# Interleaving the two output tiles of attention-times-V, and moving four x transposes to other buffers and places

## The chip, the cores and the metric

The kernel runs on one core of one Trainium2 chip. The metric is device microseconds of one execution. The profile's span is about 1.7 us shorter than the time of the same execution (339.8 us against 341.54), so spans are compared with spans and times with times. In the profile lines PE is TensorE (matmuls), PEld its weight loads, DVE VectorE, ACT ScalarE, POOL GpSimd and SP the engine that issues DMAs; L354 is line 354 of the kernel. The "granted clock" is the share of full speed that TensorE was allowed, 1 being all of it.

## The reference

Sliding-window attention (window 32, 8 batches, 8 heads, 576 positions, head size 64) gives x; a gated FFN follows.

```python
def _attn_ref(q, k, v):                      # each [8, 8, 576, 64], float32
    scores = np.matmul(q, k.transpose(0, 1, 3, 2)) / np.sqrt(64)
    mask = np.abs(pos[:, None] - pos[None, :]) <= 32
    scores = np.where(mask, scores, -1e9)
    attn = softmax(scores)                   # cut: max, exp, sum
    return np.matmul(attn, v)

def _moe_ref(x, w_gate, w_val, w_out):       # x [4608, 512], d_ff 1536
    g = x @ w_gate
    silu = g * (1.0 / (1.0 + np.exp(-g)))
    return (silu * (x @ w_val)) @ w_out
```

## The kernel before

The tokens are cut into 9 chunks of 512. For each chunk j the kernel runs FFN1 (96 matmuls with a 128x512 output into `gv_ps`), then FFN2 (48 into `ob`, in eight half-steps of six), and slips the attention of the next tokens between the half-steps. Attention works on "pairs": two blocks of 64 queries. `pair_scores` computes scores and their exponential, VectorE multiplies by the mask, `pair_av` multiplies by V, VectorE normalises to x, and `pair_xt` turns x round for the next FFN1, by a DMA transpose or, at the start of the kernel, by TensorE.

```python
ps_a = ...  # 2 buffers of two PSUM banks: scores, gv_ps, the second AV of two ("score buffers")
ps_c = ...  # 1 buffer of two banks: AV
ps_o = ...  # 2 buffers of one bank: ob, and x transposes by TensorE ("output buffers")

def pair_av(m, pool=None):
    p = pts.pop(m)
    o = (pool or ps_c).tile([128, 2, 512], FP32, ...)
    for i in range(2):                       # i: which of the two query blocks
        b, t = divmod(2 * m + i, NT)
        for h in range(H):
            nc.tensor.matmul(
                out=o[64 * i:64 * i + 64, h // 4, 66 * (h % 4):66 * (h % 4) + 66],
                lhsT=p[:, place(b, h)[0], i, place(b, h)[1], :],
                rhs=v16[b % 2][:, t, h, :], start=True, stop=True)
    ...                                      # VectorE: reciprocal, multiply -> x16s[m]

def pair_xt(m, on_pe=False):
    ...
    if not on_pe:
        nc.sync.dma_start_transpose(out=dst, in_=x16)
        return
    tp = ps_o.tile([128, GS, 128], FP16, tag="o", name="xt_ps")
    for g in range(GS):
        nc.tensor.transpose(out=tp[:, g, :], in_=x16[:, 128 * g:128 * g + 128], identity=ident)
    cast_act(dst, tp)                        # ScalarE copy to SBUF

# end of FFN2 of chunk 0
ffn2_sub(0, 2, 0); pair_scores(8); ffn2_sub(0, 2, 1)
pair_av(6); pair_av(7, ps_a)
ffn2_sub(0, 3, 0)
pair_xt(4, True)
ffn2_sub(0, 3, 1)                            # the last half-step; then osb <- ob on ScalarE
pair_xt(5, True); pair_xt(6, True); pair_xt(7, True)
pair_av(8, ps_a)
pair_xt(8)
```

(`...` marks cuts.) A "bank" in this text is 128x512 float32 of PSUM as this program allocates it: half of a score buffer or of the AV buffer, or one output buffer. With i outside, all eight matmuls that write output partitions 0 to 63 come first in the program, then the eight that write 64 to 127. The first group is called tile A below, the second tile B. Each matmul of AV uses 128 rows and 64 columns of the array (`128*64` in the lines of the trace, where an FFN matmul has `128*128`).

## Time and profile before

| | before |
|---|---|
| time, median of three runs (lowest to highest) | 341.29 us (341.18 to 341.92) |
| span of the profiled execution | 339.8 us |
| TensorE busy | 96% of the span |
| TensorE in the chain that ended last | 94% |
| granted TensorE clock | 0.995 |

The page of the kernel before, the busy line of its part 1 and the chain of its part 4 (shares of the span by engine, then by engine, tile and line):

```profile
PE 327.0 (96%) x2592; PEld 159.8 (47%) x2592; DVE 157.9 (46%) x288; ACT 155.9 (46%) x223; POOL 106.6 (31%) x139
...
PE 94%; DVE 1%; ACT 1%; DMA 1%; issue 1%; POOL 0%; POOLq 0%
PE gv_ps L391 55%; PE ob L405 27%; PE o_ps L354 4%; PE s_ps L306 3%; PE warm L437 2%; PE qk_ps L281 1%; ACT xT L262 1%; DMA xT<-x_1758 1%; PE ob L424 1%; DVE p_t L344 1%; DVE v_103 L265 0%; PE xt_ps L378 0%; DVE mask L202 0%; ACT osb L413 0%; DVE osb_4022 L265 0%
```

TensorE binds nearly everywhere, so a microsecond of TensorE work is worth up to a microsecond. AV (`o_ps`) is 4% of the chain. But "busy" does not tell whether those matmuls overlap; the order of starts does.

The timeline of TensorE before, around the AV of pairs 4 and 5 (start in us, duration, engine, line, operation, output<-inputs, count; neighbours are merged). In pair 4 the two tiles read different V buffers, so they can be told apart: tile A reads `v_103`, tile B `v_104`:

```profile
50.84 0.34 PE L354 MATMUL o_ps<-v_103,p_t 128*64 128x66 f16 x5
51.00 0.22 PE L354 MATMUL o_ps<-v_104,p_t 128*64 128x66 f16 x1
51.02 0.20 PE L354 MATMUL o_ps<-v_103,p_t 128*64 128x66 f16 x1
51.05 0.20 PE L354 MATMUL o_ps<-v_104,p_t 128*64 128x66 f16 x1
51.06 0.19 PE L354 MATMUL o_ps<-v_103,p_t 128*64 128x66 f16 x1
51.09 0.19 PE L354 MATMUL o_ps<-v_104,p_t 128*64 128x66 f16 x1
51.09 0.19 PE L354 MATMUL o_ps<-v_103,p_t 128*64 128x66 f16 x1
51.12 0.64 PE L354 MATMUL o_ps<-v_104,p_t 128*64 128x66 f16 x21
51.69 1.47 PE L405 MATMUL ob<-wo_128,hT 128*128 128x512 f16 x6
```

Five matmuls of tile A start alone, then the last three of A and the first three of B start in alternation. So in this trace the two tiles already run at once in part, for three matmuls of eight. Tile B's first matmul (51.00 us) starts ahead of tile A's sixth, seventh and eighth (51.02, 51.06 and 51.09 us), which stand before it in the kernel's loops: across the two tiles the order of starts was not the program's here.

The timeline at the end of the first FFN2, before (only TensorE, ScalarE and VectorE lines are copied; the bracket is idle time and what ended it):

```profile
57.12 0.69 DVE L363 TENSOR_TENSOR x_910<-o_ps,rall 128x512 f16<-128x512 f32 x1
...
57.22 1.46 PE L405 MATMUL ob<-wo_128,hT 128*128 128x512 f16 x6
57.42 0.60 ACT L262 ACTIVATE xT<-xt_ps 128x512 f16<-128x512 f16 x1 [1.52 <-PE xt_ps L378]
...
58.51 0.39 PE L378 MATMUL xt_ps<-ident,x_834 128*128 128x128 f16 x4
...
59.07 0.60 ACT L413 ACTIVATE osb<-ob 128x512 f32<-128x512 f32 x1 [1.06 <-PE xt_ps L378]
59.56 1.66 ACT L262 ACTIVATE xT<-xt_ps 128x512 f16<-128x512 f16 x3
59.72 0.38 PE L378 MATMUL xt_ps<-ident,x_890 128*128 128x128 f16 x4 [0.82 <-ACT osb L413]
...
61.28 1.02 PE L391 MATMUL gv_ps<-xT,wg_126 128*128 128x512 f16 x4 [0.15 <-ACT xT L262]
```

`x_910` is the normalised x of pair 7 (ready at 57.12 + 0.69 = 57.81 us), `x_834` that of pair 5, `x_890` that of pair 6. After the last half-step ScalarE copies the output (`osb`), then three turned x tiles, while TensorE mostly waits; FFN1 of chunk 1 starts at 61.28 us.

### The profile page before, as it was taken

The page shows a single profiled execution, that of the slowest core. Times are in us where ns is not written, and L with a number is a line of the kernel's source. Part 1 is how long each engine was busy: PE and PEld are TensorE (multiplying, and loading weights), DVE is VectorE, ACT ScalarE, POOL GpSimd, SP SyncE. Part 2 cuts the span into 40 slices and gives each one's busy share as a digit, 9 for nine tenths or more (in the row PEclk, how much of TensorE's full clock was granted, in tenths as well). Part 3 has the DMA queues.
Part 4 walks back from the last instruction along what each step waited for, and adds up shares of the span by engine and source line. Part 5 has one row for each costly group of instructions (what it writes and reads, how often), then busy time and mean ns, then how long its engine had stood idle before and what let it go on. Part 6 is the DMA issues. An engine that isn't in the chain of part 4 may idle for free.

```text
span 339.8 us, 6448 instructions
## 1 busy us (share of the span) xinstructions
PE 327.0 (96%) x2592; PEld 159.8 (47%) x2592; DVE 157.9 (46%) x288; ACT 155.9 (46%) x223; POOL 106.6 (31%) x139
## 2 busy tenths in 40 slices
PE   6889999999999999999999999999999999999993
PEld 3444545444544454445444454455445544444442
DVE  3744365336624763466345644564446634403310
ACT  2964576535543464337333743373336443223321
POOL 8973875146204710463045503560000000000000
PEclk9999999999999999999999999999999999999997
DMA  7999999799969996999599949998530420020012
GB/s 274 169 212 301 212 158 200 126 131 111 147 148 149 99 136 138 131 129 129 151 125 127 130 122 130 152 108 150 111 62 33 106 65 1 33 93 0 2 63 70
DMA packets 152981, 41.92 MB, mean 123 GB/s; under 512 B 140528, under 2 KB 146416, under 8 KB 152944
## 3 DMA queue, kind: packets, MB, share of 16 engines
q0 software_dynamic: 100640, 16.52, 67.7%
q1 hardware_dynamic: 52304, 24.92, 31.4%
q8 instruction: 22, 0.36, 0.5%
q14 instruction: 15, 0.12, 0.1%
HBM read 37.75 MB, written 9.44 MB: 139 GB/s over the span
## 4 chain that ended last, share of the span: by engine, by line
PE 94%; DVE 1%; ACT 1%; DMA 1%; issue 1%; POOL 0%; POOLq 0%
PE gv_ps L391 55%; PE ob L405 27%; PE o_ps L354 4%; PE s_ps L306 3%; PE warm L437 2%; PE qk_ps L281 1%; ACT xT L262 1%; DMA xT<-x_1758 1%; PE ob L424 1%; DVE p_t L344 1%; DVE v_103 L265 0%; PE xt_ps L378 0%; DVE mask L202 0%; ACT osb L413 0%; DVE osb_4022 L265 0%
## 5 line engine op out<-in xcount | busy, mean ns | idle before, releaser
L398 DVE TENSOR_TENSOR hT<-ssb,gv_ps 128x512 f16<-128x512 f16 x108 | 74.3, 688 | 122.4 <-ACT ssb L397 122.1
L397 ACT ACTIVATE ssb<-gv_ps 128x512 f16<-128x512 f32 x108 | 64.5, 597 | 112.7 <-PE gv_ps L391 110.4
L391 PE MATMUL gv_ps<-xT,wg_126 128*128 128x512 f16 x432 | 110.8, 379 | 1.2 <-ACT xT L262 0.8
L391 PE MATMUL gv_ps<-xT,wv_127 128*128 128x512 f16 x432 | 110.9, 379 | 0.0
L405 PE MATMUL ob<-wo_128,hT 128*128 128x512 f16 x420 | 97.3, 380 | 0.0
L391 PEld LDWEIGHTS <-wv_127 128*128 128x128 f16 x432 | 42.3, 98 | 51.0
L391 PEld LDWEIGHTS <-wg_126 128*128 128x128 f16 x432 | 41.9, 98 | 51.6 <-issue 2.8
L405 PEld LDWEIGHTS <-hT 128*128 128x128 f16 x420 | 38.6, 98 | 43.6
L223 POOL DMA_DIRECT2D tok<-in_q_dram x30 | 25.4, 847 | 83.3 <-DMA qT_101<-tok 45.9
L312 ACT ACTIVATE p_t<-s_ps 128x1024 f16<-128x1024 f32 (+1 forms) x40 | 35.3, 937 | 12.3 <-PE s_ps L306 12.2
L413 ACT ACTIVATE osb<-ob 128x512 f32<-128x512 f32 x35 | 21.0, 600 | 41.7 <-PE ob L405 40.6
L223 POOL DMA_DIRECT2D tok<-in_k_dram x30 | 25.3, 843 | 21.3 <-DMA kT_99<-tok 5.0
L322 DVE TENSOR_TENSOR p_t<-p_t,mask 128x1024 f16<-128x1024 f16 x32 | 22.1, 692 | 13.8 <-ACT p_t L312 13.8
L354 PEld LDWEIGHTS <-p_t 128*64 128x64 f16 x576 | 15.4, 110 | 10.6 <-issue 5.9
L361 DVE RECIPROCAL rall<-o_ps 128x8 f32<-128x8 f32 x36 | 7.3, 204 | 21.1 <-PE o_ps L354 21.0
L437 PE MATMUL warm<-mask 128*128 128x512 f16 x26 | 8.9, 467 | 2.9 <-DVE mask L202 2.9
L242 POOL DMA_DIRECT2D v_103<-in_v_dram x12 | 11.4, 956 | 0.5 <-issue 0.5
L354 PE MATMUL o_ps<-v_103,p_t 128*64 128x66 f16 x288 | 10.1, 197 | 1.1 <-DVE p_t L344 1.1
L242 POOL DMA_DIRECT2D v_104<-in_v_dram x12 | 10.6, 896 | 0.0
L397 ACT ACT_TABLE_LOAD x8 | 10.3, 1283 | 0.1
L265 DVE COPY v_103<-v_103 64x512 f16<-64x512 f16 x26 | 9.9, 381 | 0.8
L265 DVE COPY v_104<-v_104 64x512 f16<-64x512 f16 x28 | 9.4, 335 | 0.9
(137 smaller groups left out, 156.3 us busy)
## 6 DMA issues: line engine op xcount, KB each, us to landing
out_dram<-osb SPq DMA_DIRECT2D x35, 256.0 KB, 2.4
tok<-in_q_dram POOLq DMA_DIRECT2D x24, 128.0 KB, 4.9
tok<-in_k_dram POOLq DMA_DIRECT2D x24, 128.0 KB, 5.0
qk_st<-in_q_dram SPq DMA_DIRECT2D x4, 576.0 KB, 6.9
qk_st<-in_k_dram SPq DMA_DIRECT2D x4, 576.0 KB, 8.7
v_103<-in_v_dram POOLq DMA_DIRECT2D x12, 128.0 KB, 5.4
wo_128<-in_moe_w_out_dram POOLq DMA_DIRECT2D x4, 384.0 KB, 21.3
v_104<-in_v_dram POOLq DMA_DIRECT2D x12, 128.0 KB, 4.2
```

The costliest lines, as they stand in the source:

```text
L223: nc.gpsimd.dma_start(out=t[0:n].rearrange("p (h d) -> p h d", d=D), in_=src[b].rearrange("h s d -> s h d")[128 * m:128 * m + n])
L242: nc.gpsimd.dma_start(out=dst[:, 2 * m, :, 0:D], in_=src[128 * m - 32:128 * m + 96])
L265: nc.vector.tensor_copy(out=o, in_=i)
L312: nc.scalar.activation(out=o, in_=s, func=AF.Exp, bias=0.0, scale=1.0 / float(D) ** 0.5)
L322: nc.vector.tensor_tensor(out=flat, in0=flat, in1=mask, op=ALU.mult)
L354: nc.tensor.matmul(out=o[64 * i:64 * i + 64, h // 4, 66 * (h % 4):66 * (h % 4) + 66], lhsT=p[:, place(b, h)[0], i, place(b, h)[1], :], rhs ...
L391: nc.tensor.matmul(out=gv[:, i, :], lhsT=w[:, g, 128 * fk:128 * fk + 128], rhs=xts[j][:, g, :], start=(g == 0), stop=(g == GS - 1))
L397: nc.scalar.activation(out=ssb, in_=gv[:, 0, :], func=AF.Silu, bias=0.0, scale=1.0)
L398: nc.vector.tensor_tensor(out=hts[j][:, fk, :], in0=ssb, in1=gv[:, 1, :], op=ALU.mult)
L405: nc.tensor.matmul(out=ob, lhsT=hts[j][:, fk, 128 * sub:128 * sub + 128], rhs=wo16[:, fk, :], start=(fk == 0), stop=(fk == FKS - 1))
L413: nc.scalar.activation(out=osb, in_=ob, func=AF.Copy, bias=0.0, scale=1.0)
L437: nc.tensor.matmul(out=ob, lhsT=mf[:, 0:128], rhs=mf[:, 0:512], start=True, stop=True)
```

## The change

It has two parts. Part 1: the loop over the two tiles goes inside the loop over heads, so the program alternates A, B, A, B, and both tiles should run at once throughout. Part 2: at the end of the first FFN2, four x transposes go through the score buffers, two of them ahead of the last half-step (before, it was one), and one of the four copies moves to VectorE, to shorten ScalarE's tail. The AV of pair 8 moves to the AV buffer to make room.

```diff
-        for i in range(2):
-            b, t = divmod(2 * m + i, NT)
-            for h in range(H):
+        for h in range(H):
+            for i in range(2):
+                b, t = divmod(2 * m + i, NT)
                 nc.tensor.matmul(
                     out=o[64 * i:64 * i + 64, h // 4, 66 * (h % 4):66 * (h % 4) + 66],
...
-    def pair_xt(m, on_pe=False):
+    def pair_xt(m, on_pe=False, pool=None, cast=None):
...
-        tp = ps_o.tile([128, GS, 128], FP16, tag="o", name="xt_ps")
+        pool, tag = pool or (ps_o, "o")
+        tp = pool.tile([128, GS, 128], FP16, tag=tag, name="xt_ps")
...
-        cast_act(dst, tp)
+        (cast or cast_act)(dst, tp)
...
     ffn2_sub(0, 3, 0)
-    pair_xt(4, True)
+    pair_xt(4, True, (ps_a, "a"))
+    pair_xt(5, True, (ps_a, "a"))
     ffn2_sub(0, 3, 1)
-    pair_xt(5, True)
-    pair_xt(6, True)
-    pair_xt(7, True)
-    pair_av(8, ps_a)
+    pair_xt(6, True, (ps_a, "a"))
+    pair_xt(7, True, (ps_a, "a"), cast_dve)
+    pair_av(8)
     pair_xt(8)
```

## The prediction

> **What bounds it.** TensorE. PE is 96% busy (page), 94% of the chain of waits; the granted clock is 0.995. FFN matmuls (128x512, 216 ns from start to start) own 82% of the chain, AV (the o_ps matmuls) 4.4%.
>
> **Part 1, alternating AV tiles.** In the trace, instruction by instruction, the eight matmuls of one tile start 31.5 ns apart (the first two steps are 52 and 36 ns). The second tile, which writes the other 64 output partitions, starts when the first is at its sixth matmul; from there both run at once, starts 2 ns apart, each still at 31.5 ns. So a tile already costs 159 ns, not 252. From the first weight load to the next kind of matmul, one pair alone takes 0.532 us, two pairs in a row 0.850 us, of which 0.122 us is the drain at the end. [...] Alternating should make the whole block run like that overlap: about 0.37 us for one pair, 0.62 us for two. That is 0.16 us off each of 10 single blocks and 0.23 us off each of 13 double ones, 4.5 us in all. New: both tiles write the same PSUM bank at once; [...] no run here has shown it.
>
> Not all of it reaches the end:
> - Prologue (pairs 0-3): VectorE normalises back to back; 0.25 of 0.45 us stays.
> - Before the third FFN1 PE already waits 0.33 us for a DMA transpose of x (chain: 3.5 us from issue), which hangs on the first pair's normalisation; 0.3 us of 0.6 is lost. Before the second I estimate 0.1 us of slack: 0.15 lost.
> - The later four stages have over 1 us of DMA slack: 0.54 or 0.61 us each, 2.3 us together.
>
> **Part 2, end of the first FFN2.** Before, after the half-step (last matmul about 58.3 us) ScalarE runs osb, then three x copies of 0.56 us, and FFN1 starts at 61.28 us; PE idles some 1.4 us. The change takes two copies off that tail. But the transpose of pair 5 now takes the score buffer that AV of pair 7 used, so it waits until VectorE has normalised pair 7, at 57.81 us, where PE would be ready at about 56.8. VectorE is late because pair 8's mask waits for ScalarE's exp; faster AV does not help. I expect a new PE stall of about 1 us before the last half-step; then 0.3 (transpose) + 1.3 (half-step) + 0.4 + 0.6 (osb) + 0.5 (copy): FFN1 at about 61.2 in the old frame. Part 2 eats most of AV's gain in this stage (0.6 us); net +0.1.
>
> Sum: 0.25 + 0.1 + 0.4 + 0.3 + 2.3 = 3.4 us: **337.8 us**, 8 in 10 between 336.2 and 339.6. Faster by over 2%: 0.04; within 2%: 0.95; slower: 0.01.
>
> **What would show it.** o_ps blocks of 0.37 and 0.62 us, tiles starting in pairs; PE xt_ps waiting for VectorE about 1 us, FFN1 for the x DMA about 0.6 us instead of 0.3; FFN1 stages unchanged at 20.8 us.
>
> **What would make it wrong.** Same-bank writes serialise (then about 341.3); another pitch; pair 7 normalised earlier than I think (part 2 then gains up to 1 us); the slow DMA transpose of 2.25 us in that stage takes 1.2 like the others.

(0.25 + 0.1 + 0.4 + 0.3 + 2.3 is 3.35, called 3.4 us. That the whole block would run like the overlap of three matmuls in the trace before is the author's estimate.)

## The result, and the profile after

| | before | after |
|---|---|---|
| time, median (lowest to highest) | 341.45 us (341.18 to 341.92) | 338.10 us (338.04 to 338.21) |
| span of the profiled execution | 339.8 us | 336.5 us |
| ratio | | 0.9901, 95% interval 0.9884 to 0.9918 |

(The median of the kernel before is now of four runs, so it is not the 341.29 us above.) A ratio is the mean time of one kernel's fast runs over that of the other's of the same rounds, so it is not quite the ratio of the medians quoted. The change saves about 3.35 us, 1%.

The page after, the same lines:

```profile
PE 321.8 (96%) x2592; PEld 154.4 (46%) x2592; DVE 157.5 (47%) x289; ACT 155.6 (46%) x222; POOL 106.3 (32%) x139
...
PE 87%; DMA 4%; ACT 3%; DVE 3%; issue 1%; SPq 1%; ACTq 0%
PE gv_ps L392 56%; PE ob L406 24%; PE o_ps L354 3%; PE s_ps L306 3%; DMA qk_st<-in_k_dram 2%; DMA xT<-x 2%; ACT xT L262 1%; ACT p_t L312 1%; DVE x L363 1%; PE qk_ps L281 1%; DVE p_t L344 1%; PE ob L425 1%; ACT v L262 1%; SPq L215 0%; PE warm L438 0%
```

TensorE is busy 5.2 us less, but 3.3 us reach the end. Not all of the 5.2 us is the change's: AV's own busy time is 18.1 us in experiment 2, which has the old loops, and 14.0 after, so about 4.1 us of it; warm-up and transposing matmuls of the prologue differ as well (`warm` 8.9 us before, 8.3 after). TensorE's share of the chain falls from 94% to 87%. Part of that fall is new waits, for VectorE, ScalarE and the DMA transposes; 2 points of it are the input load in the prologue (`qk_st`), which landed later in this execution (10.22 us after the span's start, 9.70 before) and is in no way changed.

The same two stretches of TensorE's and the other engines' timeline, after:

```profile
50.83 0.70 PE L354 MATMUL o_ps<-v,p_t 128*64 128x66 f16 x32
51.47 1.47 PE L406 MATMUL ob<-wo,hT 128*128 128x512 f16 x6
```

```profile
57.11 0.69 DVE L363 TENSOR_TENSOR x<-o_ps,rall 128x512 f16<-128x512 f32 x1
57.86 0.40 PE L379 MATMUL xt_ps<-ident,x 128*128 128x128 f16 x4 [0.93 <-DVE x L363]
58.09 1.46 PE L406 MATMUL ob<-wo,hT 128*128 128x512 f16 x6
...
59.63 0.60 ACT L414 ACTIVATE osb<-ob 128x512 f32<-128x512 f32 x1 [0.74 <-PE ob L406]
...
60.03 0.42 DVE L265 COPY xT<-xt_ps 128x512 f16<-128x512 f16 x1 [2.23 <-PE xt_ps L379]
60.13 0.59 ACT L262 ACTIVATE xT<-xt_ps 128x512 f16<-128x512 f16 x1
...
60.77 1.02 PE L392 MATMUL gv_ps<-xT,wg 128*128 128x512 f16 x4 [0.40 <-ACT xT L262]
```

The AV block of two pairs runs from 50.83 to 51.47 us, 0.64 us, where it took 50.84 to 51.69, 0.85 us; in the trace the matmuls of the two tiles now start in pairs, 3 to 5 ns apart. At the tail TensorE stands 0.93 us in front of the transpose of pair 5 until VectorE has normalised pair 7, and only then runs the last half-step (58.09 us; it was 57.22 before). FFN1 starts at 60.77 us all the same.

To see where the time came from, take the start of each FFN1 from the trace and subtract:

| from this FFN1 to the next | before | after | gained | predicted |
|---|---|---|---|---|
| start of the span to chunk 0 | 21.48 | 21.47 | 0.01 | 0.25 |
| chunk 0 (holds part 2) | 39.79 | 39.30 | 0.49 | 0.1 |
| chunk 1 | 34.64 | 34.35 | 0.29 | 0.4 |
| chunk 2 | 35.71 | 35.39 | 0.31 | 0.3 |
| chunks 3 to 6 | 139.79 | 137.57 | 2.22 | 2.3 |
| sum | | | 3.33 | 3.4 |

(Chunks are counted from 0, and so are the FFN1 in the prediction: its "third FFN1" is the one that ends the row of chunk 2, at 131.63 us before. The expectations below call chunk 1 the second chunk.)

The chain of waits of chunk 2, before and then after (start, duration, what):

```profile
125.17 0.85 PE o_ps L354 x31
126.02 0.34 PE s_ps L306 x16
126.36 1.63 PE ob L405 x8
127.98 3.51 DMA xT<-x_1758
```

```profile
124.22 0.63 PE o_ps L354 x32
124.85 0.34 PE s_ps L306 x16
125.19 1.70 PE ob L406 x8
126.89 3.50 DMA xT<-x
```

In this chunk the chain leaves TensorE for a DMA transpose of x, so what AV saves behind the transpose's issue is only waited away. The view of waits shows it (who waited for whom: us in total, times, longest). Before, and then after:

```profile
PE gv_ps L391 <- DMA xT<-x_1758: 0.3, 1, 0.3
```

```profile
PE xt_ps L379 <- DVE x L363: 0.9, 1, 0.9
PE gv_ps L392 <- DMA xT<-x: 0.8, 2, 0.6
```

The wait for the DMA transposes grew from 0.3 us to 0.8 (0.6 of it at the end of chunk 2, 0.15 at the end of chunk 1), and the first line after is the new stall of part 2, which has no counterpart before.

### The profile page after: what moved, and what is told of

It is laid out like the page before. It is cut to its first block, busy times and chain, and to the rows that moved or that the text cites. A ratio compares the mean times of both kernels' runs of the same rounds, so it can differ in the third digit from the quotient of the medians.

```text
span 336.5 us, 6449 instructions
## 1 busy us (share of the span) xinstructions
PE 321.8 (96%) x2592; PEld 154.4 (46%) x2592; DVE 157.5 (47%) x289; ACT 155.6 (46%) x222; POOL 106.3 (32%) x139
## 4 chain that ended last, share of the span: by engine, by line
PE 87%; DMA 4%; ACT 3%; DVE 3%; issue 1%; SPq 1%; ACTq 0%
PE gv_ps L392 56%; PE ob L406 24%; PE o_ps L354 3%; PE s_ps L306 3%; DMA qk_st<-in_k_dram 2%; DMA xT<-x 2%; ACT xT L262 1%; ACT p_t L312 1%; DVE x L363 1%; PE qk_ps L281 1%; DVE p_t L344 1%; PE ob L425 1%; ACT v L262 1%; SPq L215 0%; PE warm L438 0%
## 5 line engine op out<-in xcount | busy, mean ns | idle before, releaser
L392 PE MATMUL gv_ps<-xT,wg 128*128 128x512 f16 x432 | 110.8, 379 | 1.8 <-ACT xT L262 1.1
L392 PE MATMUL gv_ps<-xT,wv 128*128 128x512 f16 x432 | 110.9, 379 | 0.0
L406 PE MATMUL ob<-wo,hT 128*128 128x512 f16 x420 | 97.3, 380 | 0.0
L392 PEld LDWEIGHTS <-wg 128*128 128x128 f16 x432 | 41.9, 98 | 52.3 <-issue 3.4
L392 PEld LDWEIGHTS <-wv 128*128 128x128 f16 x432 | 42.3, 98 | 51.0
L363 DVE TENSOR_TENSOR x<-o_ps,rall 128x512 f16<-128x512 f32 x36 | 24.9, 692 | 1.2
L242 POOL DMA_DIRECT2D v<-in_v_dram x24 | 21.5, 906 | 0.3 <-PE s_ps L306 0.3
L265 DVE COPY v<-v 64x512 f16<-64x512 f16 x54 | 18.4, 341 | 1.7
L354 PE MATMUL o_ps<-v,p_t 128*64 128x66 f16 x576 | 14.0, 196 | 0.7 <-DVE p_t L344 0.7
L306 PE MATMUL s_ps<-qT,kT 64*128 64x64 f16 x576 | 12.2, 191 | 0.4 <-DVE kT L265 0.4
```

The lines of the kernel that those rows point to most:

```text
L242: nc.gpsimd.dma_start(out=dst[:, 2 * m, :, 0:D], in_=src[128 * m - 32:128 * m + 96])
L306: nc.tensor.matmul(out=s[:, e, c, :], lhsT=kT[b % 2][half, g, 64 * t:64 * t + 128], rhs=qT[b % 2][half, g, 64 * t:64 * t + 64], start=True ...
L354: nc.tensor.matmul(out=o[64 * i:64 * i + 64, h // 4, 66 * (h % 4):66 * (h % 4) + 66], lhsT=p[:, place(b, h)[0], i, place(b, h)[1], :], rhs ...
L363: nc.vector.tensor_tensor(out=x16s[m], in0=ov[:, :, :, 0:D], in1=r.unsqueeze(3).to_broadcast([128, 2, 4, D]), op=ALU.mult)
L392: nc.tensor.matmul(out=gv[:, i, :], lhsT=w[:, g, 128 * fk:128 * fk + 128], rhs=xts[j][:, g, :], start=(g == 0), stop=(g == GS - 1))
L406: nc.tensor.matmul(out=ob, lhsT=hts[j][:, fk, 128 * sub:128 * sub + 128], rhs=wo16[:, fk, :], start=(fk == 0), stop=(fk == FKS - 1))
```

## The experiments

Each kernel was run against the kernel before on the same chip, in up to five rounds. "Chunk 0" is the time from the first FFN1 to the second in the profiled execution. There is one profile of each run, but these stage times repeat well: chunk 0 is 39.30 us in all four profiles that have the changed kernel's end and no clock dip (after, and experiments 2, 4 and 6). Only chunk 2, which holds the wait for a DMA transpose, varies by itself. The kernel before ran between 340.8 and 342.3 us in these rounds, but for one run of 352.06 us (clock 0.947), which is left out of the ratios.

### 1. Alternating AV alone

```diff
 (the kernel before, with only the loops of pair_av exchanged)
```

> Alternating AV tiles alone, the end of the first FFN2 as before. Theory N (the two parts do not add, because VectorE's normalisation of pair 7 sets the floor of the new tail): o_ps blocks of 0.38 and 0.63 us, the tail of before arrives about 0.45 us earlier (FFN1 of the second chunk at about 60.8 us of the span, as in the changed kernel at 60.77), so the time is within 0.3 us of the changed kernel, 337.8 to 338.3 us. Rival theory A (the tail rearrangement by itself gives a good share of the 3.35 us, at least 0.6): this kernel is 338.7 us or slower. Also looked at: the 0.36 us between the end of the half-step and the start of osb on ScalarE in the kernel before, which the changed kernel does not have (0.04).

Measured: 338.32 us median (338.15 to 338.71), ratio 0.9904. Blocks of 0.377 us for one pair and 0.634 us for two. Chunk 0 39.36 us. So part 1 by itself gives nearly all of the time: theory N holds here and rival A falls. The lag of osb behind the half-step is still there: the half-step ends at 57.08 + 1.46 = 58.54 us, osb starts at 58.93, 0.39 us later. (The expectations of this run count from the end of ScalarE's own wait, so they have 0.36 and 0.04 where the text has 0.39 and 0.08.) The lines of this kernel:

```profile
57.08 1.46 PE L405 MATMUL ob<-wo,hT 128*128 128x512 f16 x6
...
58.93 0.60 ACT L413 ACTIVATE osb<-ob 128x512 f32<-128x512 f32 x1 [1.05 <-PE xt_ps L378]
```

### 2. The new end of the first FFN2 alone

```diff
 (the changed kernel, with the loops of pair_av as before)
```

> The new end of the first FFN2 alone, AV in the old order. Theory N: pair 7 is still normalised at about 57.8 us (it hangs on ScalarE's exp of pair 8, not on AV), PE waits there about 0.7 us instead of 0.93, and FFN1 of the second chunk starts at about 60.8 us against 61.28: gain 0.4 to 0.6 us, 340.8 to 341.0 us where before is 341.4. Then the gains of the two parts alone sum to more than the gain of both. Rival A (parts add): this gain is what the changed kernel gains over AV alone. Rival B (the stall eats all of it): no gain, 341.4.

Measured: 340.89 us median (340.77 to 342.39), ratio 0.9989 (0.9970 to 1.0007: not clear of no change by itself). The profile is clear: chunk 0 39.30 us against 39.79, a gain of 0.49 us; pair 7 is normalised at 57.14 + 0.69 = 57.83 us, TensorE waits for it 0.5 us (0.7 was expected), and FFN1 starts at 60.80 us. In chunk 0 part 1 alone gives 0.43 us and part 2 alone 0.49 us, but both together give 0.49 us: the parts do not add there. Faster AV only makes TensorE arrive earlier at the same wait, 0.93 us instead of 0.49. The line of that wait here:

```profile
57.89 0.40 PE L379 MATMUL xt_ps<-ident,x 128*128 128x128 f16 x4 [0.49 <-DVE x L363]
```

Counted from the first FFN1, pair 7 is normalised after 36.33 us before (57.81 - 21.48), after (57.80 - 21.47), here (57.83 - 21.50) and with AV alone (58.11 - 21.78): faster AV does not move it.

### 3. Another buffer for the transpose of pair 5

```diff
-    pair_xt(5, True, (ps_a, "a"))
+    pair_xt(5, True)
```

> The changed kernel, but the transpose of pair 5 writes the output buffer of the FFN2 pool that is free, not the score buffer of AV of pair 7. Theory N: the wait of 0.93 us of the x transposes for VectorE goes, the last half-step starts about 0.9 us earlier, FFN1 of the second chunk at about 59.9 us instead of 60.77: 337.2 us, 0.9 us under the changed kernel. Rival C (another wait ends at the same time: pair 7's own transpose needs its normalisation at 57.81 us, or ScalarE's osb): the gain is under 0.3 us.

Measured: 337.05 us median (336.64 to 337.88), ratio 0.9862. Chunk 0 38.20 us instead of 39.30: 1.1 us gained where 0.9 was expected. The lines of this kernel's timeline that answer to those above:

```profile
56.73 0.61 PE L379 MATMUL xt_ps<-ident,x 128*128 128x128 f16 x8
...
57.18 1.46 PE L406 MATMUL ob<-wo,hT 128*128 128x512 f16 x6
57.29 0.69 DVE L363 TENSOR_TENSOR x<-o_ps,rall 128x512 f16<-128x512 f32 x1
58.47 0.61 PE L379 MATMUL xt_ps<-ident,x 128*128 128x128 f16 x8
...
59.85 1.02 PE L392 MATMUL gv_ps<-xT,wg 128*128 128x512 f16 x4 [0.40 <-ACT xT L262]
```

Both early transposes run at once, without a wait, and the half-step starts (57.18 us) before VectorE has normalised pair 7 (57.29 + 0.69 = 57.98 us). The stall of the changed kernel was only the choice of buffer: the transpose needed nothing of pair 7 but the place where AV of pair 7 lay.

### 4. AV in runs of four

```diff
-        for h in range(H):
+        for h4 in range(0, H, 4):
             for i in range(2):
                 b, t = divmod(2 * m + i, NT)
+                for h in range(h4, h4 + 4):
```

> The changed kernel with AV in runs of four matmuls of a tile instead of one by one. Theory W (TensorE takes a matmul of the other tile as soon as only some five instructions of the first tile's run are still waiting, which is why runs of eight overlapped by three): runs of four overlap nearly whole, blocks of about 0.40 and 0.66 us, time within 0.7 us over the changed kernel. Rival (each change of tile costs a fixed share, 3 of 8 overlapped): a run of four overlaps by three at its ends only once per change, blocks nearer 0.45 and 0.73 us, time 1.5 us or more over the changed kernel.

Measured: 339.04 us median (338.64 to 339.60), ratio 0.9920. Blocks of 0.403 and 0.662 us; chunks 3 to 6 are 0.08 or 0.09 us longer each than in the changed kernel. By its ratio this kernel is 0.65 us slower than the changed one (0.9920 against 0.9901), within the 0.7 expected; by medians it is 0.94 us, and in the profile 0.8 us lie ahead of the first FFN1 (22.30 us against 21.47), where the input load landed later still. The numbers are those of theory W: runs of four of a tile overlap nearly whole, where runs of eight (0.532 and 0.850 us) overlapped by three matmuls. The mechanism in that theory, that TensorE takes a matmul of the other tile once some five instructions of a run still wait, is the estimate from the traces; no run shows it by itself.

### 5. The changed kernel again

> The changed kernel itself, on the same chip as the three that follow, to compare with. About 338.1 us and 0.99 of the kernel before.

Measured: 338.58 us median (338.00 to 340.03), ratio 0.9900. The profiled execution is the one of 340.03 us, and it shows where the odd slow run comes from: chunk 0 took 40.98 us instead of 39.30. The view of stretches, this execution (length; busy time and count of PE, PEld, DVE, ACT and POOL; the granted TensorE clock, 1.00, 0.70 and 0.88; then the DMA's share and GB/s):

```profile
16.00:20.00 4.00, 3.10 (x72) 2.17 (x72) 3.86 (x10) 3.09 (x6) 4.00 (x6) 1.00 1.21 180
20.00:24.00 4.00, 3.12 (x15) 1.24 (x13) 0.37 (x5) 2.71 (x4) 2.95 (x5) 0.70 1.31 204
24.00:28.00 4.00, 4.00 (x18) 1.73 (x17) 1.25 (x2) 1.20 (x2) 0.03 (x1) 0.88 1.16 304
```

The clock record of the trace has one stretch of 3.4 us at half clock, at the start of the first FFN1. The view agrees: the clock not granted is 0.30 of one stretch of 4 us and 0.12 of the next, 1.7 us together, which is the difference of 40.98 and 39.30. Why the dip falls in some executions and not in others, no run here shows. It was seen in 2 of the 13 profiles, both of kernels with alternating AV. Whether the change makes it more frequent was not tested.

### 6. An earlier AV in chunks 1 and 2

```diff
             at_a, at_s = groups.get(slot, ((), ()))
+            if j in (1, 2):
+                at_a = {4: (1,), 5: (2,)}.get(slot, at_a)
...
-                pair_av(m, ps_a if i else None)
+                pair_av(m, ps_a if i or (slot == 5 and j in (1, 2)) else None)
```

> The changed kernel, and in the second and third chunk (j = 1 and 2) the AV of the second pair moves one half-step earlier, so that the DMA transposes of x that the next FFN1 waits for start about 0.6 us earlier. Theory D (what AV gained in these two chunks was lost in the wait for the DMA transpose, 0.2 and 0.6 us): the two waits go or shrink to under 0.2 us, splitting a double block into two single ones costs 0.12 us twice, net 0.4 to 0.6 us under the changed kernel. Rival (the transpose only takes longer, or waits on the queue): no gain, or slower by the 0.24 us of the split.

Measured: 338.26 us median (337.55 to 338.43), ratio 0.9897, which beside 0.9900 in the same rounds does not tell a gain of this size from none. The profile does: chunk 1 34.26 us (34.36 in the changed kernel of these rounds) and chunk 2 34.93 us (35.37), 0.53 us together, and no wait of TensorE for a DMA transpose is left. One profile would not be enough here, for that wait varies; but the three profiles with this edit (this one and two in experiment 7) all have 34.93 or 34.94 us in chunk 2, while seven of the eight profiles with faster AV and without it have 35.37 to 35.67 us, and one (experiment 9) 34.89. So in these two chunks the gain of AV had gone into that wait, as theory D says, though the timed runs alone do not prove the 0.53 us.

### 7. Both repairs

```diff
 (the changed kernel with the edits of 3 and 6)
```

> Both repairs: the transpose of pair 5 in the free output buffer, and the earlier AV of the second pair in the second and third chunk. If the two act in different stages they add: 0.9 + 0.5 = 1.4 us under the changed kernel, 336.7 us. If the slow DMA transpose only moves, 1.0 us or less.

> The kernel with both repairs once more, for a firmer time: 336.6 to 337.0 us in executions whose TensorE clock does not dip at the first FFN1, 1.7 us more in those where it does (3.4 us at half clock, seen in two profiles so far).

Measured: 337.30 us median (336.56 to 338.50), ratio 0.9860, and again 337.03 us (336.60 to 338.49), ratio 0.9872, where the changed kernel has 0.9900 and 0.9901. The first profiled execution (338.50 us) holds the other clock dip: chunk 0 39.89 us. The second does not: 38.20, 34.26 and 34.93 us in chunks 0 to 2, the gains of 3 and 6 side by side. This version beats both kernels, by 1.4 and 1.0 us against the changed one as the ratios have it (1.4 was expected). The times do not tell it from experiment 3 alone (0.9862): the share of the edit of 6 shows in the profiles only.

### 8. The lag of osb: not the neighbouring bank

```diff
 (alternating AV, the old end)
-    pair_xt(5, True)
+    pair_xt(5, True, (ps_a, "a"))
```

> AV alternating and the end of the first FFN2 in the old order, but the transpose of pair 5, which directly follows the last half-step, writes a score buffer instead of the other output buffer. Theory P (the 0.39 us from the end of the half-step to the start of osb on ScalarE, against 0.08 in the changed kernel, comes from that transpose writing the neighbouring bank of the pair of output buffers): osb starts 0.08 us after the half-step and FFN1 of the second chunk about 0.3 us earlier than with AV alone. Rival Q (it comes from something else, a transpose right behind the half-step in whatever bank): still 0.39 us, time as with AV alone.

Measured: 338.52 us median (338.23 to 338.58), ratio 0.9901. The half-step ends at 57.04 + 1.46 = 58.50 us and osb starts at 58.89: still 0.39 us. Theory P falls.

### 9. The lag of osb: one more instruction ahead of it

```diff
 (alternating AV, the old end)
     nc.scalar.activation(out=dummy, in_=rall[0:1, 0, 0:1], func=AF.Exp, bias=0.0, scale=1.0)
+    nc.scalar.activation(out=dummy, in_=rall[0:1, 0, 0:1], func=AF.Exp, bias=0.0, scale=1.0)
```

> AV alternating with the old end of the first FFN2, and one more 1x1 instruction on ScalarE some 12 us earlier, which does nothing but move every later ScalarE instruction by one place in its stream. Theory S (the 0.39 us from the end of the half-step to osb is a stall of ScalarE at a fixed place of its instruction stream; in the new end another instruction stands there, and hides it in a wait): osb starts 0.08 us after the half-step, FFN1 of the second chunk about 0.3 us earlier than with AV alone. Rival (it belongs to the order of work): still 0.39 us.

Measured: 337.73 us median (337.58 to 338.90), ratio 0.9893; chunk 0 39.05 us instead of 39.36. The lines of this kernel's timeline:

```profile
56.99 1.46 PE L405 MATMUL ob<-wo,hT 128*128 128x512 f16 x6
...
58.53 0.60 ACT L413 ACTIVATE osb<-ob 128x512 f32<-128x512 f32 x1 [0.74 <-PE ob L405]
```

The half-step ends at 58.45 us and osb starts at 58.53, 0.08 us later. A kernel that does strictly more is faster by 0.3 us in this chunk. Before and with AV alone, the bracket behind osb names the transposes of pair 5 as what ended its wait; here osb starts before they are done (58.28 + 0.39 = 58.67 us), so it does not need them. (In chunk 2 this profile has 34.89 us where AV alone has 35.38: the DMA transpose that FFN1 waits for landed 3.0 us after its issue, not 3.5, and kept TensorE waiting under 0.1 us, not 0.58. That landing takes 3.0 to 3.8 us in the 13 profiles; whether the edit has a part in it is not shown.) The lag therefore does not belong to the order of work or to a semaphore: one more place in ScalarE's instruction stream removes it, as theory S says. The other profiles fit: the lag is 0.39 or 0.40 us in the three where osb has the old place in the stream (before, experiments 1 and 8) and 0.08 us in the ten where it stands one place later. What stalls ScalarE there is not shown; in the trace of the kernel before, where the lag runs from 58.68 to 59.07 us, the DMA queues of kind `instruction` have packets that start at 54.8 and at 60.4 us and none between.

### 10. The last x copy back on ScalarE

```diff
-    pair_xt(7, True, (ps_a, "a"), cast_dve)
+    pair_xt(7, True, (ps_a, "a"))
```

> The changed kernel with the x copy of pair 7 back on ScalarE. Both last copies then stand behind osb on ScalarE: FFN1 of the second chunk 0.5 us later (one copy of 0.55 to 0.6 us, the first of them overlapping by 0.1), 338.6 us where the changed kernel is 338.1. Rival (the VectorE copy hides nothing, because osb and the first copy end later anyway): no difference.

Measured: 338.58 us median (338.42 to 339.10), ratio 0.9909; chunk 0 39.79 us instead of 39.30. The copy on VectorE is worth 0.49 us in the profile, as expected; the ratios, 0.9909 beside 0.9901, are too close to show it by themselves.

## Why the prediction was right or wrong

The time was right (337.8 us predicted, 338.1 measured), and so were most terms of its sum; the two that were off, chunk 0 (0.39 us too low) and the prologue (0.24 us too high), partly cancelled, which is luck.

- **AV blocks**: 0.37 and 0.62 us predicted; 0.377 and 0.634 us measured in the kernel with AV alone, whose loops are the same. The changed loops write both tiles to one bank at once, which no run had shown before; the blocks are as short as the overlap of the kernel before had promised, so no cost of it shows.
- **Chunks 3 to 6**: 2.3 us predicted, 2.22 measured. The kernel before already contained the evidence for this: three overlapped matmuls of eight, with steps of 29, 35 and 32 ns from start to start in tile A during the overlap, and of 52, 36, 33 and 31 ns before it.
- **Chunks 1 and 2**: 0.7 predicted, 0.60 measured, and experiment 6 shows in the profile that the rest was lost in the wait for the DMA transposes.
- **The prologue**: 0.25 predicted, 0.01 measured. Most of this is the input load, which landed early in the profiled execution before (9.70 us) and not in the other twelve (9.98 to 10.89 us, 10.08 in experiment 2 with its old loops). Counted from the start of the mask of the last heads of pairs 0 and 1 on VectorE (15.51 us before, 15.67 after) to FFN1, it is 5.97 against 5.80 us: 0.17 us gained. Experiment 2 too has 5.97, and nine of the eleven profiles with changed loops have 5.78 to 5.80 (the other two, whose load landed late, 6.09).
- **The new stall in part 2**: about 1 us predicted at the transpose of pair 5, 0.93 measured, ended by VectorE as foretold. Experiments 2 and 3 confirm its cause, and that faster AV does not help.
- **The size that was off** is the term "0.4" in "0.3 (transpose) + 1.3 (half-step) + 0.4 + 0.6 (osb) + 0.5 (copy): FFN1 at about 61.2". It measured 0.08 us, and FFN1 came at 60.77. The trace before has 0.39 us between half-step and osb, and the prediction carried it over as if it were a latency of that hand-over. It was a stall tied to a place in ScalarE's stream (experiment 9). In the changed kernel osb follows one more copy in that stream, so it stands one place later, and the stall does not show; that it is hidden there in the wait that precedes osb is argued, not shown. The printed sum does not close either: from 57.81 us its terms, 3.1 us, end at 60.9, not at 61.2. Term by term the trace after has 0.29 (transpose), 1.46 (half-step), 0.08, 0.60 (osb), 0.49 (copy) and 0.05 us to FFN1: the 0.4 was 0.32 too large and the 1.3 for the half-step 0.16 too small, so the terms by themselves would have missed by little, and for the wrong reason. That "net +0.1" for chunk 0 became +0.49 us is so in part the lag of osb and in part a total larger than its terms.

What part 2 is worth follows from this. Chunk 0 takes 39.36 us with AV alone and 39.30 with both parts, which looks like a small gain. With the accidental stall out of the way (experiment 9) AV alone takes 39.05 us, less than the changed kernel. The rearrangement of the tail loses more to the buffer it waits for than it wins by the copy on VectorE; with the right buffer (experiment 3) it would have won 39.05 - 38.20 = 0.85 us.

## What to carry to other kernels

If two groups of matmuls use different columns of the array, look at the order of their starts in the trace: when only the ends of the groups overlap, try alternating them in the program (here 0.532 and 0.850 us became 0.377 and 0.634), and cost the gain from the overlap that is already there. When work is moved into another buffer, ask who held that buffer last and when that holder is done, not only when the data is ready (here it cost 0.93 us). Before a gap in the trace is taken into a sum as a fixed latency, compare it with the same hand-over elsewhere; here a steady chunk of the same trace (half-step from 94.53 for 1.47 us, osb at 96.09) had 0.09 us where the tail had 0.39.
